# A third seven-product quad in groups 7 and 8 of a fused attention and GEGLU kernel, with a new order of their weight sums and output products

## The chip, the cores and the metric

The kernel runs on one core of a Trainium2 chip. The metric is the device time of one launch in microseconds (us). The kernel before was timed three times: 324.16 us in the median, 323.65 and 324.44 at the ends. A separate profiled execution, from which every row below is taken, took 324.89 us, and its trace spans 323.1 us.

## The reference

Two operators run one after the other. The first is causal attention over a sliding window of 128 keys with a linear distance penalty (ALiBi), for 8 batches, 8 heads, 576 positions and 64 dimensions a head:

```
scores = q k^T / 8 - slope[h] * |i - j|,   kept where 0 <= i - j < 128
attn   = softmax(scores);   x = attn v
```

Its output is laid out as 4608 tokens of 512 features. The second is a GEGLU block on those tokens:

```
out = (gelu(x @ w_gate) * (x @ w_val)) @ w_out      # 512 -> 1536 -> 512, exact gelu
```

Inputs and output are float32; the matmuls in the kernel take bf16 and accumulate in float32.

## The kernel before, in words

**Groups and blocks.** The 4608 tokens are cut into 9 groups (g = 0 to 8) of 512 tokens. The 1536 hidden features are 12 blocks of 128 (f = 0 to 11). For each group the kernel computes the hidden tile `hT` from the attention output `xT`, block by block, and then the output product of `hT` with `wo`. The attention of a later batch is interleaved with the groups: while group g is worked on, batch g + 1 gets its sums and batch g + 2 its scores. Batch 7, the last, is finished in the output stage of group 6, so groups 7 and 8 hold no attention at all.

**Order of the work.** There is no automatic scheduler here: the kernel is written under a manual schedule. Each engine takes its instructions strictly in the order in which the Python code emits them, and a semaphore wait holds up everything behind it on the same engine. TensorE (PE) does matmuls, ScalarE (ACT) copies out of the accumulators and evaluates exp and gelu, VectorE (DVE) does additions and multiplications that read accumulators, GpSimd (POOL) does additions on SBUF data and issues most loads, and SyncE (SP) issues stores, transposing DMAs and the small relays between two halves of an accumulator bank.

**Plain blocks.** `gate_val` (L628) computes one block of one group: four matmuls of 512 columns for the gate, four for the value, one gelu on ACT (L649), one multiplication on DVE (L650).

**Quads.** `gate_quad` (L805) computes four blocks at once with a seven-product scheme (Strassen's, in Winograd's form). It takes the two weight matrices as a 2 by 2 matrix (gate and value, each cut into two halves of the 512 features) and the tokens as a 2 by 2 matrix (the same halves, and two halves of 256 tokens). Seven products of 8 matmuls with 256 columns take the place of eight. The inner function `P(n)` issues product n for two pairs of blocks, u = 0 and 1. The order on PE is P(1), P(2), P(6), P(5), P(7), P(3), P(4). In between, ACT copies P(1), the sum in x and P(5) out of the accumulators (L843, L849, L852) and evaluates the gelu of two halves (L836); DVE adds into these copies (`add_to`, L833: after P(2), after P(7), after P(3)) and multiplies the lower token half (L866); POOL multiplies the upper token half (L870, L872). A quad holds six of the eight accumulator banks: two called x, two z and two y. Its staging space and gelu space come from tiles that are no longer in use (`rooms`, L794).

**Sums that a quad needs.** `combine_weights(f0)` (L755) makes four sums of weights with eight additions. Those for blocks 6 to 9 are made once and stay in `kept`; those for blocks 0 to 3 are made by POOL during the output stage of group 6 and lie in the probabilities' space `Ps[0]`. `combine_x(g)` (L777) makes four sums of tokens with four additions. Group 7's are made in two parts, tokens 0 to 191 early by DVE, and tokens 192 to 255, which need the end of batch 7, by POOL in the output stage of group 6 (L1192).

**Output products.** `out_products` (L1142) uses the same scheme for `hT` times `wo`, again seven products, here of 6 matmuls for each half a = 0, 1 of the group's lower 256 tokens; `product` (L735) issues one. The sums of hidden values come from `combine_left` (L712), in four kinds: 0 and 1 give the left factors of products 5 and 6, 3 that of product 7, 2 that of product 3. `gather_out` (L885) takes the products out: copies on ACT (named p1, u2, p5, c21), additions on DVE (c11, c22, c12). Product 4 accumulates on top of the bank that c22 reads.

**Groups 7 and 8 before.** Quad 0 (blocks 0 to 3), plain blocks 4 and 5, quad 6 (blocks 6 to 9), plain blocks 10 and 11, and then all output products in a row, with `combine_left` spread over POOL and DVE.

**Batch 3.** `spread_dma` (L447) reads the reciprocals of the row sums back from DRAM and spreads them over partitions. For batch 3 it is issued on ACT's queue, after block 11 of group 2; for the others by SP after block 6.

**The start.** `keep_busy` (L73) runs matmuls on zeros while the first inputs arrive (L1018).

## Time and profile before

| | before |
|---|---|
| median of 3 runs | 324.16 us (323.65 to 324.44) |
| profiled execution | 324.89 us, of which the trace spans 323.1 us |
| PE busy | 313.5 us, 97% of the span |
| DVE busy | 249.2 us, 77% |
| ACT busy | 219.5 us, 68% |
| POOL busy | 197.0 us, 61% |
| granted TensorE clock | 1.00 in every slice |
| group 7, hidden blocks | 262.96 to 282.09 us of the span |
| group 7, output products | 282.09 to 291.29 us |
| group 8, hidden blocks | 291.29 to 310.42 us |
| group 8, output products | from 310.42 us |

How to read it. The trace has one row for each stretch of like instructions on an engine: start and length in us from the span's beginning, the engine, the line of the kernel, the operation, what it writes and reads, shapes, and how often. A bracket behind it gives the time that the engine had idled and what ended the wait. Matmuls are pipelined and the end of each is modelled, so a row of n matmuls is somewhat longer than the time to the next row's start; starts are the better measure. The chain of waits follows the work back from the last instruction, at each step to what released it. The 1.79 us between the span and the execution's time lie outside the trace.

### The profile page before, as it was taken

The numbers are of one execution on the slowest core, as the hardware profiler recorded it, in microseconds if no ns is written. First come the engines' busy times: TensorE is split into PE (matmuls) and PEld (weight loads), VectorE is DVE, ScalarE is ACT, GpSimd is POOL, SyncE is SP. The second block draws the span as 40 slices with busy tenths as digits, with TensorE's granted clock in tenths as the row PEclk, the third lists the DMA queues.
The fourth block names the chain that finished last, engine by engine and source line by source line (L and its number), as shares of the span: only waits on it lengthen the run. The fifth ranks groups of instructions, "written<-read, shape, count | busy, mean of one in ns | idle before, by whom it ended". The sixth has DMA issues, their size and how long they took to land.

```text
span 323.1 us, 9359 instructions
## 1 busy us (share of the span) xinstructions
PE 313.5 (97%) x3712; PEld 212.5 (66%) x3742; DVE 249.2 (77%) x493; ACT 219.5 (68%) x421; POOL 197.0 (61%) x228
## 2 busy tenths in 40 slices
PE   8889999999999999999999999999999999999995
PEld 3565746466454768566855786578747787788764
DVE  7769776978779887976798679877897756895692
ACT  7973678647979679657966787578767256627641
POOL 5974589385096885579945995496009496410450
PEclk9999999999999999999999999999999999999999
DMA  7999999999999959995999699949204230003003
GB/s 210 166 194 192 200 178 181 139 178 191 161 147 164 138 101 181 191 142 153 179 193 158 162 168 190 148 124 179 102 36 103 49 132 0 2 0 132 0 4 130
DMA packets 149920, 43.57 MB, mean 135 GB/s; under 512 B 133588, under 2 KB 142964, under 8 KB 149876
## 3 DMA queue, kind: packets, MB, share of 16 engines
q0 software_dynamic: 107456, 18.10, 75.9%
q1 hardware_dynamic: 41424, 23.35, 33.1%
q10 hardware_dynamic: 996, 1.53, 2.1%
q8 instruction: 29, 0.48, 0.6%
q14 instruction: 15, 0.12, 0.1%
HBM read 43.65 MB, written 9.53 MB: 165 GB/s over the span
## 4 chain that ended last, share of the span: by engine, by line
PE 91%; ACT 3%; issue 2%; DMA 1%; DVE 1%; SPq 0%; ACTq 0%; DVEq 0%
PE ps L643 36%; PE ps L745 20%; PE ps L825 19%; PE ps L494 5%; PE ps L679 4%; PE ps L304 2%; PE ps L699 2%; PE ps L218 1%; DMA qs<-in_q_dram 1%; ACT P L233 1%; PE ps L432 1%; PE ps L156 1%; SPq L938 0%; DVE xT L533 0%; ACTq L449 0%
## 5 line engine op out<-in xcount | busy, mean ns | idle before, releaser
L643 PE MATMUL ps<-xT,wv 128*128 128x512 bf16 (+3 forms) x303 | 71.3, 354 | 0.2
L643 PE MATMUL ps<-xT,wg 128*128 128x512 bf16 (+3 forms) x290 | 68.8, 353 | 1.6 <-issue 0.6
L649 ACT ACTIVATE gelu<-ps 128x512 bf16<-128x512 f32 (+3 forms) x77 | 41.6, 546 | 41.5 <-PE ps L643 38.5
L650 DVE TENSOR_TENSOR hT<-ps,gelu 128x512 bf16<-128x512 f32 (+3 forms) x77 | 46.3, 623 | 18.4 <-PE ps L643 14.7
L233 ACT ACTIVATE P<-ps 128x512 bf16<-128x512 f32 (+1 forms) x108 | 52.5, 577 | 6.2 <-PE ps L304 3.0
L643 PEld LDWEIGHTS <-wv 128*128 128x128 bf16 x308 | 28.9, 98 | 30.8 <-DVE xT L553 1.4
L643 PEld LDWEIGHTS <-wg 128*128 128x128 bf16 x308 | 28.4, 98 | 26.7 <-issue 0.7
L238 DVE TENSOR_TENSOR P<-P,emask 128x768 bf16<-128x768 bf16 x60 | 31.9, 553 | 6.8 <-ACT P L233 5.1
L745 PEld LDWEIGHTS <-hT 128*128 128x128 bf16 x336 | 32.1, 98 | 6.3 <-issue 0.5
L114 POOL DMA_DIRECT2D vb<-in_v_dram x40 | 33.9, 878 | 3.7 <-DMA wo<-in_moe_w_out_dram 1.0
L870 POOL TENSOR_TENSOR hT<-qT,qs 128x512 bf16<-128x512 f32 x10 | 11.5, 1167 | 26.5 <-ACT qs L836 26.5
L114 POOL DMA_DIRECT2D ks<-in_k_dram x30 | 25.4, 886 | 3.4 <-DMA qs<-in_q_dram 3.2
L825 PEld LDWEIGHTS <-kept 128*128 128x128 bf16 x256 | 25.1, 98 | 2.9
L1332 POOL COPY mark<-hT 1x2 bf16<-1x2 bf16 x5 | 0.9, 174 | 42.7 <-DVE hT L650 42.7
L114 POOL DMA_DIRECT2D qs<-in_q_dram x30 | 25.4, 863 | 1.7 <-DMA wo<-in_moe_w_out_dram 0.9
L745 PEld LDWEIGHTS <-left 128*128 128x128 bf16 x252 | 24.1, 98 | 3.4 <-DVE left L720 0.2
L745 PE MATMUL ps<-right,hT 128*128 128x256 bf16 x168 | 22.2, 273 | 0.3 <-ACT osb L894 0.3
L833 DVE TENSOR_TENSOR qT<-ps,qT 128x512 f32<-128x512 f32 x20 | 12.9, 686 | 12.2 <-PE ps L825 10.9
L745 PE MATMUL ps<-wo,hT 128*128 128x256 bf16 x168 | 21.2, 273 | 0.0
L833 DVE TENSOR_TENSOR P<-ps,P 128x512 f32<-128x512 f32 x24 | 15.0, 682 | 7.1 <-PE ps L825 7.1
L745 PE MATMUL ps<-right,left 128*128 128x256 bf16 x168 | 20.4, 273 | 0.0
L494 PE MATMUL ps<-P,vb 64*64 64x192 bf16 (+2 forms) x752 | 17.5, 221 | 1.7 <-issue 1.5
(173 smaller groups left out, 615.7 us busy)
## 6 DMA issues: line engine op xcount, KB each, us to landing
out_dram<-osb SPq DMA_DIRECT2D x34, 256.0 KB
rb<-rd SPq DMA_DIRECT2D x8, 576.0 KB
vb<-in_v_dram POOLq DMA_DIRECT2D x32, 128.0 KB, 7.1
qs<-in_q_dram POOLq DMA_DIRECT2D x24, 128.0 KB, 6.1
ks<-in_k_dram POOLq DMA_DIRECT2D x24, 128.0 KB, 7.3
wo<-in_moe_w_out_dram POOLq DMA_DIRECT2D x4, 384.0 KB, 12.2
wg<-in_moe_w_gate_dram POOLq DMA_DIRECT2D x5, 256.0 KB, 7.8
wv<-in_moe_w_val_dram POOLq DMA_DIRECT2D x5, 256.0 KB, 8.4
```

Source lines behind the costliest of these rows:

```text
L114: nc.gpsimd.dma_start(out=t[at:at + n, j, :].rearrange("p (h d) -> p h d", h=H), in_=src[b][:, 128 * j:128 * j + n, :].rearrange("h p d -> ...
L233: nc.scalar.activation(out=dst, in_=src, func=AF.Exp, scale=0.125)
L238: nc.vector.tensor_tensor(out=dst, in0=dst, in1=m, op=ALU.mult)
L494: mm = nc.tensor.matmul(out=out, lhsT=lhsT, rhs=prob(b)[half, c, i, col:col + q1 - q0], start=all(t[2] != u for t in todo[:n]), stop=True, ...
L643: nc.tensor.matmul(out=ps, lhsT=w[:, c, 128 * f:128 * (f + 1)], rhs=xT[:, c, t0 + lo:t0 + hi], start=begins, stop=(c == 3), skip_group_che ...
L649: nc.scalar.activation(out=gl[:, 0:n], in_=pg, func=AF.Gelu)
L650: nc.vector.tensor_tensor(out=hid[g][:, f, lo:hi], in0=pv, in1=gl[:, 0:n], op=ALU.mult)
L679: nc.tensor.matmul(out=acc[g], lhsT=hid[g][:, f, 128 * t:128 * (t + 1)], rhs=wo[:, f, :], start=(f == 0), stop=(f == NF - 1))
L745: nc.tensor.matmul(out=made[g, a, into], lhsT=lhsT, rhs=rhs, start=first and i == 0, stop=i == NF // 2 - 1, skip_group_check=True)
L825: nc.tensor.matmul(out=ps[:, 256 * e:256 * e + 256], lhsT=w[:, c, at:at + 128], rhs=x[:, c, :], start=n in (1, 2, 5) and e == 0 and c == 0 ...
L833: nc.vector.tensor_tensor(out=to[u], in0=cut(banks[n, u], to[u].shape[1]), in1=to[u], op=ALU.add)
L870: nc.gpsimd.tensor_tensor(out=out, in0=P5[u], in1=high, op=ALU.mult)
```

## The change

- **Groups 7 and 8** compute quad 6 first, then quad 0, then a third quad that takes blocks 4, 5, 10 and 11 in place of the four plain blocks. The constant `PAIRS` says which blocks make up a quad.
- The third quad's **weight sums** (`combine_weights(4)`, eight additions) are made by POOL in group 7, three before quad 6 and five after it, in the space of `Ps[1]`, and used again in group 8. It has staging space of its own, and its upper token half is multiplied by DVE instead of POOL (`high=nc.vector`), after both lower multiplications. Between its first and second additions DVE makes the sums of kinds 0 and 1 for blocks 6 to 9 (`between`).
- **Output products of groups 7 and 8**: products 1, 2, 6 and 5 are each issued in two parts, first for the pairs of blocks 0, 1, 3, 4 (in the old quads) and then for 2 and 5 (in the third quad). All sums of kinds 3 and 2 go to DVE. In group 7 `combine_x` for group 8 comes after product 7 instead of after product 6.
- **Output stage of group 6**: `combine_x` for tokens 192 to 255 goes from POOL to DVE, behind c11 of a = 1.
- **Batch 3**: its spread is issued by POOL after block 6, ahead of the loads of batch 5. In group 2 the exp table is loaded before the copy p1, as in the later groups.
- **Groups 2 to 5**: half of one addition into `T` (the second of the two of part 0) moves behind the scaling of the previous batch's values.
- **The start**: 2 matmuls of 128, 7 of 512 and 2 of 128 columns on zeros in place of 8 of 512.

```diff
-QUADS = (0, 6)
+PAIRS = {0: (0, 2), 6: (6, 8), 4: (4, 10)}
...
-            (nc.scalar if b == 3 else nc.sync).dma_start(
+            (nc.gpsimd if b == 3 else nc.sync).dma_start(
                 out=recip[b][64 * i:64 * i + 64, :, :],
...
     def gate_quad(g, f0, room=None, between=None, high=nc.gpsimd):
...
+        if high is nc.vector:
+            low(0)
+            low(1)
         for u in (0, 1):
+            if high is not nc.vector:
+                low(u)
...
-    keep_busy(held[0], 8, 512, zeros[:, 0:1].to_broadcast((128, 512)))
+    keep_busy(held[0], 2, 128)
+    keep_busy(held[0], 7, 512, zeros[:, 0:1].to_broadcast((128, 512)))
+    keep_busy(held[0], 2, 128)
...
         if b > B:
+            early, late = (0, 1, 3, 4), (2, 5)
+            def both(n, which=range(NF // 2), *after):
+                for a in (0, 1):
+                    P(n, a, which)
+                    for what in after:
+                        O(what, a)
+                store()
+            both(1, early)
+            both(2, early)
+            both(1, late, "p1")
+            both(2, late)
+            combine_left(g, 2, 6, (0, 1), step=3)
+            both(6, early)
+            both(5, early)
+            combine_left(g, 0, 6, (3,))
+            both(6, late, "u2", "c11")
+            both(5, late, "p5")
+            combine_left(g, 0, 6, (2,))
+            both(7, range(NF // 2), "c22")
+            if g + 1 < NG:
+                combine_x(g + 1)
+                both(3, range(NF // 2), "c12")
+                both(4, range(NF // 2), "c21")
...
-            combine_x(g + 1, 192, 256, engine=nc.gpsimd)
             for do in sums[4:]:
                 do()
             O("c11", 1)
+            combine_x(g + 1, 192, 256)
             P(6, 1)
...
-        if g == 2:
-            O("p1", 0)
         exp_table()
-        if g > 2:
-            O("p1", 0)
+        O("p1", 0)
...
-        add(b, 0, None, (0,))
+        add(b, 0, None, (0,), (0,))
...
+        add(b, 0, None, (0,), (1,))
...
         if g >= B - 1:
+            sums = combine_weights(4) if g == B - 1 else []
+            for do in sums[:3]:
+                do()
+            gate_quad(g, 6)
+            store()
+            for do in sums[3:]:
+                do()
+            gate_quad(g, 0)
+            combine_left(g, 0, 2, (0, 1), engine=nc.gpsimd)
+            gate_quad(g, 4, (wide_of([(kT[1], 2), (vb[0], 2), (vb[1], 2)]), tiles_of([(qs[1], 4)])),
+                      lambda: combine_left(g, 3, 5, (0, 1)), high=nc.vector)
             out_products(g)
...
-            if f == (11 if g == 2 else 6):
+            if f == 6:
                 spread_dma(g + 1)
```

More of the change, by code (lines that the diff above doesn't have):

```diff
@@ L377, in scores0_rest, with add @@
                           emask[:, 2 * c:2 * c + 2, 0:192].unsqueeze(2).to_broadcast((128, 2, 2, 192))))
-    def add(b, c0, copy=None, what=(0, 2, 1)):
+    def add(b, c0, copy=None, what=(0, 2, 1), halves=(0, 1)):
         hs = slice(2 * c0, 2 * c0 + 4)
@@ L385, in add @@
         if 0 in what:
-            for x in (0, 1):
+            for x in halves:
                 half = slice(64 * x, 64 * x + 64)
@@ L710, in halves, with combine_left @@
         return hid[g].rearrange("p (i e) (h t) -> p i e h t", e=2, h=2)
-    def combine_left(g, lo, hi, which=(0, 1, 2, 3), engine=nc.vector):
-        x, ns = halves(g), slice(lo, hi)
+    def combine_left(g, lo, hi, which=(0, 1, 2, 3), engine=nc.vector, step=1):
+        x, ns = halves(g), slice(lo, hi, step)
         a11, a12, a21, a22 = (x[:, ns, e, h, :] for h in (0, 1) for e in (0, 1))
@@ L733, with product @@
     made = {}
-    def product(g, n, a, lo=0, hi=NF // 2):
+    def product(g, n, a, which=range(NF // 2)):
         (l, r), into = FACTORS[n], INTO[n]
-        first = n in (1, 2, 5)
+        count = made.get((g, a, n), 0)
+        first = n in (1, 2, 5) and not count
+        made[g, a, n] = count + len(which)
         if first:
@@ L741, in product @@
         x = wo.rearrange("p (i e) (h t) -> p i e h t", e=2, h=2)
-        for i in range(lo, hi):
+        for k, i in enumerate(which):
             lhsT = left[:, l, i, cols] if isinstance(l, int) else halves(g)[:, i, l[0], l[1], cols]
             rhs = right[:, r, i, :] if isinstance(r, int) else x[:, i, r[0], r[1], :]
-            nc.tensor.matmul(out=made[g, a, into], lhsT=lhsT, rhs=rhs, start=first and i == 0,
-                             stop=i == NF // 2 - 1, skip_group_check=True)
+            nc.tensor.matmul(out=made[g, a, into], lhsT=lhsT, rhs=rhs, start=first and k == 0,
+                             stop=count + k == NF // 2 - 1, skip_group_check=True)
     def flat_of(t):
@@ L752, with weights @@
     sums_w = {0: [flat_of(Ps[0])[:, 1024 * n:1024 * n + 1024].rearrange("p (c f) -> p c f", c=2) for n in range(4)],
+              4: [flat_of(Ps[1])[:, 1024 * n:1024 * n + 1024].rearrange("p (c f) -> p c f", c=2) for n in range(4)],
               6: [kept[:, n, :, :] for n in range(4)]}
+    def weights(w, c, f0):
+        a, b = PAIRS[f0]
+        return w[:, c, 128 * a:128 * b + 256].rearrange("p (n y) -> p n y", y=256)[:, 0:(b - a) // 2 + 1:(b - a) // 2, :]
     def combine_weights(f0, engine=nc.gpsimd):
@@ L803, in rooms, with gate_quad @@
             P[:, 4 * n:4 * n + 4, 288:416] for n in (0, 1)], tiles_of([(vb[g % 2], 4)])
-    def gate_quad(g, f0, room=None, between=None):
+    def gate_quad(g, f0, room=None, between=None, high=nc.gpsimd):
         if g not in hid:
@@ L838, in hidden @@
         def hidden(u, half):
-            return hid[g][:, f0 + 2 * u:f0 + 2 * u + 2, 256 * half:256 * half + 256]
+            f = PAIRS[f0][u]
+            return hid[g][:, f:f + 2, 256 * half:256 * half + 256]
         P(1)
@@ L1146, in out_products @@
         if b > B:
-            last = [(4, ("c21",)), (3, ("c12",))]
-            for n, after in [(1, ("p1",)), (2, ()), (6, ("u2", "c11")), (5, ("p5",)), (7, ("c22",))] + (
-                    last if g == NG - 1 else last[::-1]):
-                early = g == NG - 1 and n in (3, 4)
+            early, late = (0, 1, 3, 4), (2, 5)
+            def both(n, which=range(NF // 2), *after):
                 for a in (0, 1):
-                    if early and a == 0 and n == 4:
-                        P(3, 0, 0, 1)
-                    P(n, a, *((1,) if early and a == 0 and n == 3 else ()))
+                    P(n, a, which)
                     for what in after:
@@ L1157, in out_products @@
                 store()
-                if n == 6 and g + 1 < NG:
-                    combine_x(g + 1)
+            both(1, early)
[14 more added lines that the diff above has]
+                both(4, range(NF // 2), "c21")
+            else:
+                P(3, 0, range(1))
+                both(4, range(NF // 2), "c21")
+                P(3, 0, range(1, 6))
+                O("c12", 0)
+                store()
+                P(3, 1)
+                O("c12", 1)
+                store()
             return
@@ L1235, in out_products @@
         P(1, 1)
-        P(3, 0, 0, 2)
+        P(3, 0, range(2))
         P(4, 0)
-        P(3, 0, 2)
+        P(3, 0, range(2, 6))
         O("p1", 1)
@@ L1281 @@
         if g >= B - 1:
[L1282 to L1296 removed]
+            sums = combine_weights(4) if g == B - 1 else []
+            for do in sums[:3]:
+                do()
+            gate_quad(g, 6)
+            store()
+            for do in sums[3:]:
[4 more added lines that the diff above has]
+                      lambda: combine_left(g, 3, 5, (0, 1)), high=nc.vector)
             out_products(g)
```

42 lines of the change are left out of this document (16 added, 26 removed).

## The prediction

> **What bounds the kernel now.** I read the page first, for the engines' shares:
>
> ```profile
> span 323.1 us, 9359 instructions
> PE 313.5 (97%) x3712; PEld 212.5 (66%) x3742; DVE 249.2 (77%) x493; ACT 219.5 (68%) x421; POOL 197.0 (61%) x228
> ```
>
> Then the chain of waits from 255 us on, since most of the change lies there:
>
> ```profile
> 256.39 6.73 PE ps L745 x60
> 263.12 6.11 PE ps L825 x56
> 269.24 0.05 issue
> 269.29 3.40 PE ps L643 x15
> 272.69 6.11 PE ps L825 x56
> ...
> 282.26 9.19 PE ps L745 x84
> ```
>
> The chain is PE alone: a quad of 56 matmuls takes 6.11 us, two plain blocks 3.40 + 0.05, the 84 output matmuls 9.19, nothing between. So work taken from PE is time gained, and any wait put before a matmul is time lost in full. I work in us against the profiled execution, 324.89 (span 323.1 and 1.79 around it); it stands 0.73 above the median of 324.16, and I carry the difference over to the median.
>
> **1. The third quad: -1.6.** Four plain blocks cost 2 x 3.45 = 6.90, a quad 6.11; 0.79 a group, 1.58 in two, if PE runs the quads back to back.
>
> **2. Batch 3's spread: -0.3.** In group 2 PE waits once:
>
> ```profile
> 117.31 1.33 ACTq L449 DMA_DIRECT2D rb<-rd  x2
> 121.40 0.38 ACT L894 COPY osb<-ps 128x256 f32<-128x256 f32 x1
> 121.83 0.82 PE L745 MATMUL ps<-right,hT 128*128 128x256 bf16 x6 [0.33 <-ACT osb L894]
> ```
>
> The two issues hold ACT for 1.33; the copy u2 at 121.40 comes late by this, and PE's product 7 by 0.33. Without them the table load follows the last gelu, and the wait goes: -0.33, at least 0. On POOL two issues stand ahead of batch 5's loads. These rows tell who waits for them:
>
> ```profile
> 117.72 4.27 POOL L114 DMA_DIRECT2D qs<-in_q_dram  x5
> 135.85 4.19 SPq L177 DMA_TRANSPOSE kT<-ks  x1
> 150.29 1.33 SPq L449 DMA_DIRECT2D rb<-rd  x2
> 153.44 0.80 PE ps L304 x33
> ```
>
> Five issues take 4.27, two some 1.7. If all of this reaches SP's transposes, SP is done at 153.3 instead of 151.6, just as PE's scores of 153.44 begin, whose relays SP carries. I take 0, at most +0.3.
>
> **3. Group 6's token sums on DVE: +3.2.** The sums for tokens 192 to 255 are four additions of 128x128, put in front of c22 on DVE while POOL makes weight sums without a break:
>
> ```profile
> 256.52 2.26 POOL L761 TENSOR_TENSOR P<-wv 128x512 bf16<-128x512 bf16 x2
> 258.75 2.26 POOL L761 TENSOR_TENSOR P<-P,wg 128x512 bf16<-128x512 bf16 x2
> 260.11 0.41 DVE L896 TENSOR_TENSOR osb<-ps,osb 128x256 f32<-128x256 f32 x1
> 260.98 0.42 POOL L783 TENSOR_TENSOR ks<-xT 128x128 bf16<-128x128 bf16 x1
> 261.83 0.42 DVE L902 TENSOR_TENSOR osb<-ps,osb 128x256 f32<-128x256 f32 x1 [1.31 <-ACT osb L900]
> 262.31 0.81 PE L745 MATMUL ps<-right,hT 128*128 128x256 bf16 x6
> ```
>
> The DVE row at 261.83 is c22 of a = 1, ended at 262.25; PE's product 4, which accumulates onto the bank that c22 reads, starts at 262.31. There is no slack: what delays c22 delays PE, and behind it all of groups 7 and 8. What a DVE addition on two SBUF operands costs beside a busy POOL is seen in group 7:
>
> ```profile
> 279.36 2.32 POOL L870 TENSOR_TENSOR hT<-qT,qs 128x512 bf16<-128x512 f32 x2 [4.83 <-ACT qs L836]
> 280.33 0.34 DVE L720 TENSOR_TENSOR left<-hT 128x256 bf16<-128x256 bf16 x1
> 280.70 1.12 DVE L720 TENSOR_TENSOR left<-left,hT 128x256 bf16<-128x256 bf16 x1
> 282.80 1.15 POOL L720 TENSOR_TENSOR left<-hT,left 128x512 bf16<-128x512 bf16 x1
> 282.97 1.25 DVE L720 TENSOR_TENSOR left<-hT 128x512 bf16<-128x512 bf16 x1
> 284.26 0.42 DVE L720 TENSOR_TENSOR left<-left,hT 128x512 bf16<-128x512 bf16 x1
> 284.60 0.28 DVE L720 TENSOR_TENSOR left<-hT 128x256 bf16<-128x256 bf16 x1
> ```
>
> With POOL idle, 256 columns take 0.28 and 512 take 0.42. With POOL at work the same take 1.12 and 1.25, and end just after POOL's instruction has ended (281.82 after 281.68, 284.22 after 283.95). So the DVE addition waits for POOL's current instruction; and the addition at 280.70 came too late to follow the one at 280.33, because POOL's next had begun in between. Additions that read an accumulator (0.41 and 0.42 here, beside a busy POOL) don't wait. Now the four: c11 ends at 260.52. POOL, whose own token sums are gone, is in its fourth addition until 261.0. The first DVE addition (0.2 by the two lengths above, an estimate) ends at 261.2, and each further one waits out one POOL addition of 1.1: 262.5, 263.8, 265.1. c22 then ends at 265.5 instead of 262.25, and PE loses 3.2. This is the upper end. If the third and fourth, which need nothing that isn't ready, follow the second before POOL gets in, c22 ends at 263.2: +1.0. With no waiting at all the four take 0.8 and are done by 261.4, before c22 could start: 0. I take 3.2, since in each case seen POOL got in between.
>
> The Trainium skill (SBUF — State Buffer, section "SBUF: two separate sides") has a rule on this that speaks against the change: VectorE instructions with two SBUF inputs and GpSimd's share a pair of ports under an exclusive lock, held for a whole instruction, and the loser blocks fully. The 1.12 and 1.25 agree with it. By that rule each of the four competes anew, which is the 3.2; the gentler ordering above would need VectorE to keep the lock between two instructions.
>
> **4. Quads back to back: +0.4.** Here are ACT's and DVE's rows for quad 6, whose PE work runs from 272.53 to 278.64:
>
> ```profile
> 272.53 1.91 PE L825 MATMUL ps<-xT,wg 128*128 128x256 bf16 x16
> 274.27 2.78 PE L825 MATMUL ps<-ks,kept 128*128 128x256 bf16 x24
> 277.77 1.04 PE L825 MATMUL ps<-ks,wv 128*128 128x256 bf16 x8
> 273.22 1.07 ACT L843 COPY qT<-ps 128x512 f32<-128x512 f32 x2 [0.70 <-PE ps L825]
> 278.65 1.23 ACT L836 ACTIVATE qs<-kT 128x512 bf16<-128x512 f32 x2 [0.59 <-DVE kT L833]
> 274.11 1.29 DVE L833 TENSOR_TENSOR qT<-ps,qT 128x512 f32<-128x512 f32 x2 [0.62 <-PE ps L825]
> 276.73 1.29 DVE L833 TENSOR_TENSOR qT<-ps,qT 128x512 f32<-128x512 f32 x2 [1.33 <-PE ps L825]
> 279.13 1.28 DVE L866 TENSOR_TENSOR hT<-ps,qs 128x512 bf16<-128x512 f32 x2
> ```
>
> ACT's last gelu ends 1.24 after the quad does (279.88 - 278.64). The next quad's copies could start 0.69 after its own start (273.22 - 272.53) and now start at 1.24; the first ends at 1.24 + 0.54 = 1.78, and P(6), due at 1.74, needs it: about 0.1 lost with the semaphore. Two such places in each of two groups: +0.4; the lower end is 0. The plain blocks gave ACT this time before.
>
> Accumulator banks: six of eight are in use in a quad, and the two called z are free again after the first additions (275.40). So the next quad finds four, which do for P(1) and P(2), and I add nothing. If the banks are handed out in fixed turn instead, P(2) of the next quad, due 0.87 after its start, waits for the lower multiplications (279.13 and 0.6 later, ended by 280.41): the second ends 1.77 after the quad's end where PE wants it at 0.87 + 0.44 = 1.31, so 0.5 at six places (the output products of each group count too), 3.0. The code doesn't fix the turn, and I keep this as an upper end.
>
> **5. DVE's sums inside the third quad: +0.7.** `between` puts two dependent additions of 512 columns behind DVE's first pair, which ends 275.40 - 272.53 = 2.87 after a quad's start (3.1 with the lag of part 4). Alone they take 0.8 and end at 3.9, before the next pair's 4.20. But POOL then works on quad 0's upper halves (2.3 for two) and its sums (2 x 1.15). The pair of 276.73 ends 5.49 after the start and P(4)'s second half is due at 5.24 + 0.44, so 0.2 is the slack. Both additions waiting out a whole POOL instruction would end at 3.1 + 2 x 1.45 = 6.0 and cost 1.6. In group 7 POOL's five weight sums (5 x 1.12) come between quad 6's multiplications (6.8 to 9.1 after the group's start, by 279.36 - 272.53) and quad 0's, which so run from 14.7, or 2.3 in the third quad's own time, to 4.6: the second addition is held until then and ends at 4.9, a loss of 0.3 to 0.4; I take 0.3. In group 8 POOL is about to begin its sums at 3.1, and I let one of the two additions be held: 0.4. Bounds 0 and 1.6 for each group.
>
> **6. Output products: +0.2.** After the third quad DVE still has two lower and two upper multiplications (2.4 to 2.6), two sums (0.8) and then this kind twice, with two c11 (0.75) between:
>
> ```profile
> 254.50 0.95 DVE L720 TENSOR_TENSOR hT<-hT 128x1536 bf16<-128x1536 bf16 x1
> ```
>
> That is 0.5 + 2.5 + 0.8 + 0.95 + 0.75 + 0.95 = 6.5 after the quad's end; product 3 in group 8 starts after 60 matmuls of 0.109 (9.19 / 84), at 6.6. Product 7 needs the first of the pair at 5.2 and has it at 4.8. With the lateness of part 5 some tenths are lost once: +0.2, between 0 and 0.4. POOL's sums for blocks 0 to 3 are needed 2.6 or more after the quad's end and are there.
>
> **7. At nothing.** POOL's eight new weight sums (8 x 1.12) fit: POOL is free of sums before quad 6's multiplications, and the last one is due only in the third quad's P(3), some 3 us after it ends; were it late, its lateness would be the price. The half addition moves within DVE's queue while PE, behind it, has output products to do. The start:
>
> ```profile
> 1.00 3.59 PE L75 MATMUL ps<-zeros 128*128 128x512 bf16 x8 [1.00 <-DVE zeros L927]
> 4.41 0.50 PE L995 MATMUL ps<-ident,qs 128*128 128x128 bf16 x3
> ```
>
> The columns are 4096 in both; a matmul of 128 starts 0.13 after the one before (0.50 less 0.24 for the last one's length, over two), so four cost at most 0.52 where one of 512 cost 0.45: 0 to +0.07.
>
> **The sum.** -1.58 - 0.33 + 3.2 + 0.4 + 0.7 + 0.2 = +2.6: 327.5 for the profiled execution, 326.8 for the median.
>
> **The rivals.**
>
> *The lock lets DVE's later additions through* (part 3 at 1.0): -1.58 - 0.33 + 1.0 + 0.4 + 0.7 + 0.2 = +0.4, 324.6. For it: those additions are independent, unlike the pairs seen. Against: POOL had its next instruction waiting each time.
>
> *DVE isn't held*, the faster side: a DVE addition that arrives while POOL has a queue goes between at once, and POOL waits. Parts 3 and 5 fall to 0; -1.91 + 0.4 = -1.5, 322.7. It decides from the point where the four token sums stay under about 0.3 each, so that c22 starts at 261.83 as before. For it: the addition at 280.33 took only 0.34. Against: 1.12 and 1.25.
>
> *Worse*: banks in fixed turn (+3.0), or both sums of part 5 held for whole instructions in group 8 (+1.2): 328.0 to 329.8.
>
> *The third quad saves nothing*, as its PE time is hidden: the chain above excludes it, PE being the bound.
>
> **How the numbers follow.** No change that a measurement of this kernel can tell is within 0.3%, 323.2 to 325.1. Forecast 326.8 with chance 0.45, its own range 325.6 to 328.0 (parts 4 to 6 at their ends); the first rival 0.17 (same), the second 0.28 (faster), the worse ones 0.10. Slower 0.55. The range takes in the second rival and the forecast's own: 322.4 to 328.2.
>
> **What would show it.** In the changed profile: the four DVE additions on line L783's successor in group 6's output stage at about 1.1 each and a wait of PE before the last product there (part 3); 168 quad matmuls a group in about 18.5 to 19.4 us with gaps of about 0.1 where quads meet; DVE's two sums inside the third quad above 0.42 each, and a wait of P(4) on DVE; no wait on u2 in group 2. I am wrong if the four are short and PE doesn't wait there.

## The result, and the profile after

The kernel after takes 333.25 us in the median of 6 runs (332.44 to 335.50), the kernel before 324.11 beside it; the ratio is 1.028 (95% interval 1.026 to 1.030). It is slower by 9.1 us. Its profiled execution took 333.11. The page after:

```profile
span 331.3 us, 9491 instructions
...
PE 315.4 (95%) x3767; PEld 218.9 (66%) x3793; DVE 264.7 (80%) x501; ACT 225.0 (68%) x433; POOL 201.4 (61%) x230
...
PEclk9999999999999999999999999999999959999999
```

PE's share fell from 97 to 95%, and one slice of forty has half the TensorE clock. The chain of waits (start, length, what) shows where:

```profile
250.94 2.67 PE ps L747 x24
...
259.27 8.32 DVE ks L789
...
268.50 1.44 PE ps L747 x6
269.94 16.61 PE ps L836 x136
...
290.63 9.29 PE ps L747 x84
299.91 18.64 PE ps L836 x168
```

Until group 6's output products (250.94, before 252.19) the profiled run is 1.25 ahead. Then one DVE addition stands in the chain for 8.3 us. DVE's rows there, with POOL's and PE's for the same time (L789 is a token sum, L921 is c22, L767 a weight sum, L747 an output product, L836 a quad's product):

```profile
258.86 0.41 DVE L915 TENSOR_TENSOR osb<-ps,osb 128x256 f32<-128x256 f32 x1
259.19 8.39 DVE L789 TENSOR_TENSOR ks<-xT 128x128 bf16<-128x128 bf16 x1
267.61 0.22 DVE L789 TENSOR_TENSOR ks<-xT,ks 128x128 bf16<-128x128 bf16 x1
...
268.03 0.42 DVE L921 TENSOR_TENSOR osb<-ps,osb 128x256 f32<-128x256 f32 x1
...
255.27 2.25 POOL L767 TENSOR_TENSOR P<-wv 128x512 bf16<-128x512 bf16 x2
...
264.14 2.24 POOL L767 TENSOR_TENSOR P<-wv 128x512 bf16<-128x512 bf16 x2
266.35 1.14 POOL L767 TENSOR_TENSOR P<-P,wg 128x512 bf16<-128x512 bf16 x1
...
268.50 1.44 PE L747 MATMUL ps<-right,hT 128*128 128x256 bf16 x6 [7.35 <-DVE osb L921]
269.73 3.57 PE L836 MATMUL ps<-xT,wg 128*128 128x256 bf16 x16
```

The first token sum starts inside POOL's fourth weight sum and ends at 267.58, just behind the eleventh (267.49). From the lengths of its neighbours, 0.22, it was held for some 8.2 of its 8.39; the trace books all of it as DVE's busy time. The next three take 0.22 each, c22 follows, and PE, which waits for c22, has stood for 7.35. Then it is slow: product 4 takes 1.44 where before it took 0.81, the first 16 matmuls of the quad 3.57 where a quad at full speed took 1.91. In a table of stretches (from:to, length, then the busy time of PE, PEld, DVE, ACT and POOL with their counts, granted clock, DMA share, GB/s):

```profile
268.50:271.20 2.70, 2.70 (x13) 1.93 (x13) 0.28 (x1) 0.69 (x2) 0.00 (x0) 0.50 0.26 98
271.20:280.00 8.80, 8.80 (x74) 7.45 (x72) 5.79 (x10) 6.18 (x13) 1.78 (x2) 0.89 0.08 30
```

The granted clock is 0.50 after the wait, 0.89 in the next stretch, and back at 1.00 later (in 299.91:318.55). Quad 6 takes 269.73 to 277.51, that is 7.78 instead of 6.11. So the stall costs 7.35, and the slow clock (1.44 - 0.81) + (7.78 - 6.11) = 2.3 more.

The account, in us of the span, by PE's starts: -1.25 up to group 6's output products; +7.35 and +2.3; the rest of group 7's hidden blocks -0.07 (269.73 to 290.46, that is 20.73 for 19.13, less 1.67 of clock); its output products +0.09 (9.29 for 9.20); group 8's hidden blocks -0.49 (18.64 for 19.13), and its output products with the end of the span +0.23 (12.91 for 12.68). That is +8.2, as the two profiled executions differ (333.11 - 324.89).

### The profile page after: what moved, and what is told of

Its sections match the earlier page's. It is cut to its first block, busy times and chain, and to the rows that moved or that the text cites. A ratio compares the mean times of both kernels' runs of the same rounds, so it can differ in the third digit from the quotient of the medians.

```text
span 331.3 us, 9491 instructions
## 1 busy us (share of the span) xinstructions
PE 315.4 (95%) x3767; PEld 218.9 (66%) x3793; DVE 264.7 (80%) x501; ACT 225.0 (68%) x433; POOL 201.4 (61%) x230
## 4 chain that ended last, share of the span: by engine, by line
PE 91%; DVE 5%; issue 2%; ACT 1%; ACTq 0%; DVEq 0%
PE ps L643 31%; PE ps L836 22%; PE ps L747 19%; PE ps L494 5%; PE ps L679 4%; DVE ks L789 3%; PE ps L304 2%; PE ps L699 2%; PE ps L218 2%; PE ps L75 1%; PE ps L432 1%; PE ps L156 1%; DVE xT L574 0%; ACT P L233 0%; PE ps L1014 0%
## 5 line engine op out<-in xcount | busy, mean ns | idle before, releaser
L643 PE MATMUL ps<-xT,wv 128*128 128x512 bf16 (+3 forms) x271 | 63.1, 351 | 0.2
L643 PE MATMUL ps<-xT,wg 128*128 128x512 bf16 (+3 forms) x262 | 61.1, 350 | 1.3 <-issue 0.6
L649 ACT ACTIVATE gelu<-ps 128x512 bf16<-128x512 f32 (+3 forms) x69 | 36.9, 541 | 36.5 <-PE ps L643 34.3
L650 DVE TENSOR_TENSOR hT<-ps,gelu 128x512 bf16<-128x512 f32 (+3 forms) x69 | 40.7, 616 | 15.7 <-PE ps L643 12.2
L643 PEld LDWEIGHTS <-wv 128*128 128x128 bf16 x276 | 25.9, 98 | 26.4
L747 PEld LDWEIGHTS <-hT 128*128 128x128 bf16 x336 | 32.1, 98 | 13.9 <-issue 8.0
L643 PEld LDWEIGHTS <-wg 128*128 128x128 bf16 x276 | 25.2, 98 | 23.6 <-issue 0.4
L747 PE MATMUL ps<-right,hT 128*128 128x256 bf16 x168 | 23.1, 278 | 7.6 <-DVE osb L921 7.4
L836 PEld LDWEIGHTS <-kept 128*128 128x128 bf16 x256 | 25.1, 98 | 3.0
L747 PEld LDWEIGHTS <-left 128*128 128x128 bf16 x252 | 24.2, 98 | 3.5 <-issue 0.3
L836 PE MATMUL ps<-xT,wg 128*128 128x256 bf16 x192 | 24.6, 285 | 0.0
L836 PEld LDWEIGHTS <-wg 128*128 128x128 bf16 x192 | 19.6, 102 | 4.1
L747 PE MATMUL ps<-wo,hT 128*128 128x256 bf16 x168 | 21.4, 273 | 0.0
```

Of the source, the lines that this page charges most:

```text
L643: nc.tensor.matmul(out=ps, lhsT=w[:, c, 128 * f:128 * (f + 1)], rhs=xT[:, c, t0 + lo:t0 + hi], start=begins, stop=(c == 3), skip_group_che ...
L649: nc.scalar.activation(out=gl[:, 0:n], in_=pg, func=AF.Gelu)
L650: nc.vector.tensor_tensor(out=hid[g][:, f, lo:hi], in0=pv, in1=gl[:, 0:n], op=ALU.mult)
L747: nc.tensor.matmul(out=made[g, a, into], lhsT=lhsT, rhs=rhs, start=first and k == 0, stop=count + k == NF // 2 - 1, skip_group_check=True)
L836: nc.tensor.matmul(out=ps[:, 256 * e:256 * e + 256], lhsT=lhsT, rhs=x[:, c, :], start=n in (1, 2, 5) and e == 0 and c == 0, stop=c == 1, s ...
```

## The experiments

The theory after this result: while POOL has additions ready, DVE's addition on two SBUF inputs waits for the end of POOL's whole run, not for one instruction; and the slow clock follows from PE's standing. The rival is the prediction's: one POOL instruction for each DVE addition.

**The token sums back on POOL.** The old place, ahead of the second four weight sums:

```diff
+            combine_x(g + 1, 192, 256, engine=nc.gpsimd)
             for do in sums[4:]:
                 do()
             O("c11", 1)
-            combine_x(g + 1, 192, 256)
```

> The changed kernel with the four token sums of group 6's output stage back on POOL, at their old place; all else as changed. Theory (run): what cost the time is that DVE's first token sum waited 8.39 us, until POOL's run of weight sums ended, with PE behind it for 7.35, and that PE then ran 2.3 us slower at a lower clock. Then no wait of PE before product 4, clock 1.00 throughout, and 333.1 - 7.35 - 2.3 = 323.5, within 0.8 of it, since POOL is 1.7 later in group 7 and may hold up the third quad more. Rival: the third quad and its sums are the loss; then above 328.

Measured 325.82, ratio 1.007 (1.004 to 1.010). PE doesn't wait before product 4, so the stall does hang on this one move. It is 2.3 above what was expected, because POOL, with four more additions, is late in group 7, and there the two DVE sums inside the third quad wait (2.59 and 1.25). The first:

```profile
277.32 2.59 DVE L720 TENSOR_TENSOR left<-hT 128x512 bf16<-128x512 bf16 x1
```

**A run of eight.** The three early sums of the third quad go behind quad 6:

```diff
-            for do in sums[:3]:
-                do()
             gate_quad(g, 6)
             store()
-            for do in sums[3:]:
+            for do in sums:
                 do()
```

> The changed kernel with the first three weight sums of the third quad issued behind quad 6's multiplications with the other five, so that POOL's run beside DVE's token sums is 8 additions long and not 11. Theory (run): DVE's first token sum waits 3 x 1.11 = 3.3 less, 5.0 in place of 8.39, and PE waits 4.0 in place of 7.35. Rival (it waits for something else than the end of POOL's run, data or a fixed time): 8.4 and 7.35 as before. The third quad's own sums come later and may cost up to 2 there; so 330 to 332 by the first, 333 to 335 by the rival.

Measured 332.7 in two runs (331.43 and 333.97; ratio 1.025). The first token sum and PE's product 4:

```profile
258.94 5.08 DVE L789 TENSOR_TENSOR ks<-xT 128x128 bf16<-128x128 bf16 x1
...
264.93 1.44 PE L747 MATMUL ps<-right,hT 128*128 128x256 bf16 x6 [4.04 <-DVE osb L921]
```

Three sums less (3.3 us) and the wait is 3.3 shorter: the run's end decides. It gave little back in time, since the clock fell after 4.04 of standing too, and the late sums held up the third quad. (Two runs don't tell its time from that of after; the rows do tell the waits apart.)

**Gaps in the run.** Behind each weight sum POOL copies two elements of its result, so that it has to wait for itself:

```diff
+            def one(o, a, b, op):
+                engine.tensor_tensor(out=o, in0=a, in1=b, op=op)
+                if engine is nc.gpsimd:
+                    engine.tensor_copy(out=mark, in_=o[0:1, 1, 254:256])
...
```

> The changed kernel with a copy of two elements on POOL behind each of its weight sums, reading what that sum wrote, so that POOL must finish one before it goes on. Theory (run): DVE gets in at the first such gap; each token sum waits for one addition at most, the first 1.3 or less, and PE's wait before product 4 is 1 to 3.5. Rival (DVE waits until POOL has nothing at all to do): POOL's run is longer by 11 copies of about 0.3, so the first token sum waits 9 or more and PE 8 or more.

Measured 325.16, 1.004 (1.002 to 1.005). The four token sums took 0.22, 1.20, 0.21 and 1.30, and PE waited 1.2. The gaps, copies of 0.18 to 0.27, let DVE in, as the theory says; the clock stayed at 1.00.

**PE kept busy.** 34 matmuls on zeros ahead of product 4:

```diff
+            keep_busy(bank(), 34, 512, zeros[:, 0:1].to_broadcast((128, 512)))
             P(4, 1)
```

> The changed kernel with 34 matmuls of 512 columns on zeros (7.3 us) in PE's queue ahead of the last product of group 6, into a bank that nobody reads. Theory (clock): PE still can't go on before 268.5 or so, but its clock doesn't fall; product 4 takes 0.82 instead of 1.44 and quad 6 6.1 instead of 7.78, so 333.1 - 2.3 = 330.8. Rival (quad 6 is slow because its operands or sums are late): 333, with quad 6 at 7.8.

Measured 330.13 in two runs (330.25 and 330.01; ratio 1.018). DVE's wait is the same, PE's speed behind it is not:

```profile
258.56 8.41 DVE L789 TENSOR_TENSOR ks<-xT 128x128 bf16<-128x128 bf16 x1
...
268.53 1.91 PE L836 MATMUL ps<-xT,wg 128*128 128x256 bf16 x16
```

1.91 again at a granted clock of 1.00, and 3 us less in time: the slow matmuls came from PE's standing. The Trainium skill (TensorE: Matmul & The Clock Gate, section "Part 1: The HAM clock gate") says that the clock falls to half after an idle window of about 3.4 us; 7.35 and 4.04 here, and 1.2 with no fall, agree with it.

**POOL waits for the token sums.** The remedy: POOL's second four sums start only when DVE's token sums are done.

```diff
+            O("c11", 1)
+            combine_x(g + 1, 192, 256)
+            nc.gpsimd.tensor_copy(out=mark, in_=sums_x(g + 1)[3][0:1, 1, 254:256])
             for do in sums[4:]:
                 do()
-            O("c11", 1)
-            combine_x(g + 1, 192, 256)
```

> The kernel after with one new wait: POOL's second four weight sums in group 6's output products begin only when the four token sums on DVE are done (a copy of two elements on POOL that reads the last of them). The run in front of the token sums is then four additions instead of eleven. Theory that a whole run of POOL's ready additions holds DVE: the first token sum lasts until the fourth weight sum ends, 0.5 to 0.8, the others 0.22 each, PE waits 0 to 0.3 for product 4, the clock stays at 1.0, and the rest of group 7 is late only where DVE's sums inside the third quad meet POOL's sums and multiplications (1 to 2): 323.0, between 322.3 and 324. Theory of the prediction, one POOL addition for each DVE addition: with POOL idle behind its fourth sum it gives the same here, 0.5 and three short ones, so this run prices the remedy rather than tells the two apart. If instead DVE's additions on SBUF are slow beside whatever POOL does, PE waits 3 or more and the time stays above 327.

Measured 323.52, ratio 0.996 (0.994 to 0.998): 9.7 below after, and 0.4% below before, a small gain. DVE's first token sum and c22, POOL's second four sums, and the chain of waits from there:

```profile
258.42 0.65 DVE L789 TENSOR_TENSOR ks<-xT 128x128 bf16<-128x128 bf16 x1
...
259.81 0.42 DVE L921 TENSOR_TENSOR osb<-ps,osb 128x256 f32<-128x256 f32 x1 [0.21 <-issue]
...
259.80 2.26 POOL L767 TENSOR_TENSOR P<-wg,wv 128x512 bf16<-128x512 bf16 x2
```

```profile
254.37 6.73 PE ps L747 x60
261.10 14.99 PE ps L836 x136
...
280.17 9.29 PE ps L747 x84
```

All 60 output matmuls follow each other in 6.73, as before. Group 7's hidden blocks take 19.07 (261.10 to 280.17).

**The sums behind the lower multiplications.** The same, and DVE's two sums leave the middle of the third quad:

```diff
-        if between:
+        if between and high is not nc.vector:
             between()
...
             low(0)
             low(1)
+            if between:
+                between()
...
```

> As the run before, and DVE's two sums inside the third quad stand behind its two lower multiplications instead of behind its first pair of additions, so that no add of the quad is queued behind them. If part 5 of the prediction has its place right (a sum held by POOL holds DVE's next pair and with it P(4)), the third quad takes 6.2 in both groups, PE waits nowhere in groups 7 and 8 for an add into vb, and the time is 1 to 2 under the run before: 321.8, faster than both kernels. Rival: the sums are then late for product 6 (due 2.6 after the quad), and what is won in the quad is lost there: as the run before.

Measured 323.52, 0.998 (0.996 to 1.000): as the run before, so the rival holds. PE's rows at the start of each quad of group 7, of its output products and of group 8:

```profile
263.93 1.91 PE L836 MATMUL ps<-xT,wg 128*128 128x256 bf16 x16
...
270.04 1.91 PE L836 MATMUL ps<-xT,wg 128*128 128x256 bf16 x16
...
276.23 1.91 PE L836 MATMUL ps<-xT,wg 128*128 128x256 bf16 x16
...
282.40 2.78 PE L747 MATMUL ps<-wo,hT 128*128 128x256 bf16 x24
...
292.16 1.91 PE L836 MATMUL ps<-xT,wg 128*128 128x256 bf16 x16
```

By these starts the quads take 6.11, 6.19 and 6.17, 18.47 in all instead of 19.06; the third alone took 6.77 in the run before, so what it lost there came from the two sums. The products take 9.76 instead of 9.29: with the sums behind the multiplications, PE waits 0.19 for a left factor and starts late at other places. 28.23 against 28.35 in all.

**The small parts.** Two kernels on the base of before: the 11 zero matmuls alone, and these with batch 3's spread, the later p1 and the half addition.

```diff
-    keep_busy(held[0], 8, 512, zeros[:, 0:1].to_broadcast((128, 512)))
+    keep_busy(held[0], 2, 128)
+    keep_busy(held[0], 7, 512, zeros[:, 0:1].to_broadcast((128, 512)))
+    keep_busy(held[0], 2, 128)
```

> The kernel before with the 11 zero matmuls of the change alone. The profiled run of before has 1.54 us of PE standing at 15.70 to 17.24 with nothing named that it waits for; the runs of after and of the first four experiments have none, and all of them hold the new zeros. If the zeros are what takes it away, the time falls by about 1.0, to 323.2, and the first gate matmul starts at about 16.5 or earlier. If it is an accident of the one profiled run, or comes from something else in the change, the time stays within 0.3 of before, 324.2, and I price the zeros at 0 to +0.07 as in the prediction.

> The kernel before with everything of the change outside groups 6, 7 and 8: the zeros, the spread of batch 3 on POOL, p1 behind the table load, half an addition into T later. By the ledger of the profiled run of after (1.25 us ahead of before at group 6's output products) it takes 322.9, with no wait of PE on u2 in group 2 (-0.33) and a stall less of 0.3 to 0.4 at 130 us. By the prediction's parts 2 and 7 alone it takes 323.8. If the head start is an accident of single runs, 324.2.

The zeros: 0.999 (0.998 to 1.001), no difference; the 1.54 us stall at the start of the profiled run before is gone here at an equal time, and it is no fixed price of the old zeros: in five added runs with these (the five kernels of added stages below) it is 0.16 to 0.83. All small parts: 0.998 (0.996 to 1.000), or -0.7 us with an interval of -1.3 to -0.1. The kernel that waits for the token sums is another 0.3 below this by the medians. The intervals don't tell the two apart, but one profiled run of each gives the same: groups 7 and 8 take 56.33 us in it and 56.66 with the small parts alone.

**POOL and DVE alone.** Is it really the run? Stages behind the end of the kernel before, with nothing else at work: POOL gets six ready instructions (eight in the next two runs), DVE comes in between, in most stages after a copy out of an accumulator; the first copy lets POOL start. Of these runs only the rows count, and each was profiled once.

```diff
+    def phase(kind, wait, adds, n=6):
...
+        nc.vector.tensor_copy(out=kf[0:1, 0:2], in_=last[0:1, 0:2])
+        for i in range(n):
...
+            nc.gpsimd.tensor_tensor(out=out, in0=a, in1=kf[:, 0:512], op=ALU.mult if kind == "f32" else ALU.add)
...
+        for _ in range(wait):
+            nc.vector.tensor_copy(out=flat_of(qT[1]).bitcast(FP32)[:, 0:512], in_=spare)
+        for i in range(adds):
+            nc.vector.tensor_tensor(out=slot(kT[0], i, 256), in0=slot(vb[0], i, 256), in1=slot(vb[1], i, 256), op=ALU.add)
```

> The kernel before with eight short stages added at its end, which compute nothing of the output (some 60 us; the time itself is of no use). In each, POOL runs six instructions of 128x512 that are ready from the start, and DVE comes in between with additions of 128x256 on SBUF, most of them after one copy out of an accumulator (0.7), so that they arrive inside POOL's first instruction. POOL's six are additions bf16 with bf16 that don't depend on each other, multiplications f32 with bf16 like the upper halves of a quad, or additions each of which reads the one before. Theory 1, a run of ready POOL instructions holds DVE whatever they are: about 6 us for one DVE addition beside the independent additions and beside the multiplications, at most 1.3 beside the chain, whose links leave gaps; four DVE additions behind each other take the end of the run and three times 0.25. Theory 2, only the bf16 additions hold on, the multiplications let DVE in at each boundary (as at 286.63 of after, 0.85): 6 us beside the additions, 1.3 or less beside the multiplications. Theory 3, the prediction's, one POOL instruction for each DVE addition everywhere: 0.5 to 1.3 in each stage. If what counts is when DVE arrives, the stages without the copy ahead (DVE there at about the same moment as POOL) differ from those with it.

The theory fell. In no stage did DVE wait out more than one POOL instruction at a time, whatever POOL did (in the two without the copy it was there ahead of POOL). Four DVE additions beside six independent bf16 additions:

```profile
342.56 4.32 DVE L1397 TENSOR_TENSOR kT<-vb,vb 128x256 bf16<-128x256 bf16 x4
```

That is 1.08 each, which is the prediction's rule.

> The kernel before with twelve stages added at its end, which compute nothing of the output (the time itself is of no use). The last run went against my theory: there DVE got in after one POOL instruction in every stage, while in group 6 of after it waited out seven. So something else than POOL's being ready decides. The stages put the parts of group 6 together again: POOL runs eight instructions, either its real weight sums, or additions of one tile with itself, or additions in two strided pieces of 256; DVE brings the real four token sums (128x128 in two pieces of 64), or four plain additions of 256 or 128 columns, or the two product sums of 512; in three stages PE runs 40 matmuls beside them, in two of these ACT 12 copies. If POOL's operands decide, all stages with the real sums hold DVE for 5 to 8 us. If DVE's do, all with the token sums. If it takes a busy PE or ACT, only those stages. If none holds it for more than 1.3, the cause is none of these, and stays open.

Neither the operands nor a busy PE or ACT makes the difference: the real token sums beside the real weight sums took 0.91, 1.07, 1.18 and 1.18, with PE and ACT at work or not, and no other stage held DVE for longer than 1.25.

> The kernel before with 24 stages added at its end, which compute nothing of the output (the time itself is of no use). In each, POOL runs its eight real weight sums and DVE brings the four token sums; only the moment at which DVE arrives inside POOL's first sum is moved, by the width of a copy (in the last eight an addition) out of an accumulator ahead of them, from about 0.35 to 1.0 us after the sum's start. In the runs of the changed kernel in which DVE was held for the whole run (after, the run of eight, the one with PE kept busy) it arrived 0.58 to 0.59 after the start of POOL's fourth sum; in the stages of the last two runs, which never held it, at 0.03 to 0.38, and at 1.03. If the moment decides, some stages, those near 0.59, hold DVE for 7 to 8 us and the others for at most 1.3. If it doesn't, none of the 24 does, and what held DVE in group 6 stays open.

Nor does the moment inside the sum: in all 24 stages, with arrivals from 0.5 to 1.0 us after the start of POOL's first sum, the first token sum ended just behind that sum. What all these stages share is that DVE comes early in the run. The next three runs try that. The second puts a copy of 0.41 between c11 and the token sums of after; the third puts one more addition into DVE's order:

```diff
             P(3, 0)
             scale[1]()
+            nc.vector.tensor_tensor(out=flat_of(ks[0])[:, 0:128], in0=wg[:, 0, 0:128], in1=wv[:, 0, 0:128], op=ALU.add)
```

> The kernel before with 14 stages added at its end, which compute nothing of the output (the time itself is of no use). POOL runs its eight weight sums (in two stages twelve additions), and DVE comes to its additions on SBUF only inside the fourth sum or later, as in group 6 of after; in three stages with the same instructions ahead as there (four multiplications out of an accumulator into the tokens, one addition out of an accumulator), so that the first token sum also waits for DVE's own last multiplication; one of these with PE and ACT at work; seven stages move the moment inside the sum; three bring other additions. If it is the late arrival, or DVE's wait for itself, that makes POOL keep the port, these stages hold DVE to the end of the run, 3 to 9 us. If none does, neither is the cause.

> The kernel after with a copy of 256 columns out of an accumulator (0.3 to 0.4) on DVE between c11 and the four token sums, so that they come later inside POOL's run and behind another instruction. If the moment inside POOL's sum decides, which is 0.58 in all runs that were held, DVE arrives at about 0.95 here and is held for at most one sum each, and the time is 326 to 328. If not, DVE is held to the end of the run again, for about 8.0, and the time stays at 333.

> The kernel after with one more addition on DVE, 128 columns of weights into a dead tile, ahead of the third scaling, some 2 us before the token sums and inside POOL's first or second weight sum. If any DVE addition on two SBUF inputs is held by this run, it waits for its end, about 10.5, and the time is 335 to 336. If one early in the run gets in after one sum, it lasts 0.3 to 1.3, and what counts is where in the run DVE arrives; then the token sums behind it show whether a first turn changes what follows.

In the first, DVE arrived in POOL's third sum in 13 of the 14 stages and in the fifth in one. Eleven stages held it to the run's end, for 3.8 to 10.3 us, all with nothing but POOL and DVE at work. Two of them, beside runs of eight and of twelve:

```profile
332.30 5.86 DVE L783 TENSOR_TENSOR ks<-xT 128x128 bf16<-128x128 bf16 x1
...
342.09 10.27 DVE L783 TENSOR_TENSOR ks<-xT 128x128 bf16<-128x128 bf16 x1
```

In the other three DVE had arrived in the last 0.14, 0.19 and 0.23 of POOL's third sum and got in behind it; four of the eleven came that late as well, so there it goes either way. In the second run the token sum was held for 8.06, so a later moment doesn't help; 331.88. The third gave 328.33: one addition *more* on DVE, 5 us less than after. DVE's rows, and PE's product 4:

```profile
256.60 0.67 DVE L1225 TENSOR_TENSOR ks<-wg,wv 128x128 bf16<-128x128 bf16 x1
...
259.45 1.15 DVE L789 TENSOR_TENSOR ks<-xT 128x128 bf16<-128x128 bf16 x1
260.63 1.08 DVE L789 TENSOR_TENSOR ks<-xT,ks 128x128 bf16<-128x128 bf16 x1
261.63 1.18 DVE L789 TENSOR_TENSOR ks<-xT 128x128 bf16<-128x128 bf16 x1
...
264.31 1.01 PE L747 MATMUL ps<-right,hT 128*128 128x256 bf16 x6 [3.51 <-DVE osb L921]
```

The added one (L1225) arrives in POOL's second sum and gets in behind it; after it the four token sums go one by one (1.15, 1.08, 1.18 and 1.18), which is the case that the prediction had priced. PE waited 3.51; the granted clock was 0.74 in product 4 (264.31:265.32) and 0.50 in the next 2.7 us.

**Which sum DVE meets.** Only the place in the run is moved.

> The kernel before with 21 stages added at its end, which compute nothing of the output (the time itself is of no use). POOL runs eight instructions (real weight sums in six stages, additions of one tile in six, f32 by bf16 multiplications in six), and DVE's four token sums arrive in the middle of POOL's first, second, third, fourth, fifth or sixth. From the runs so far: arrival in the first or second gets in after that one and the four go one by one (about 1.1 each); arrival in the third or later is held to the run's end (some 6, 5, 4 and 3 us for the third to the sixth). If this holds for the weight sums alone, the multiplications show 0.3 to 1.3 everywhere, as the upper halves in group 7 did. In the last three stages DVE brings one addition of 128 columns in the first, second or third sum and the token sums two or more sums later: if an early turn keeps the way open, as one look at the changed kernel with an early addition suggests, the token sums go one by one in the first two and the early addition itself is held in the third. If the sum that DVE meets is not what decides, held and not held mix without such an order.

The stages were meant to bring the first token sum into POOL's first to sixth weight sum of eight. A step of the delay (two copies, 1.36) is longer than a sum (1.11), so by the rows of POOL it arrived in the first, second, fourth, fifth, sixth and seventh; the third was missed. DVE's six rows, and POOL's for the stage at 341.91:

```profile
320.62 0.49 DVE L783 TENSOR_TENSOR ks<-xT 128x128 bf16<-128x128 bf16 x1
...
331.26 0.23 DVE L783 TENSOR_TENSOR ks<-xT 128x128 bf16<-128x128 bf16 x1
...
341.91 5.51 DVE L783 TENSOR_TENSOR ks<-xT 128x128 bf16<-128x128 bf16 x1
...
353.04 4.17 DVE L783 TENSOR_TENSOR ks<-xT 128x128 bf16<-128x128 bf16 x1
...
364.20 2.80 DVE L783 TENSOR_TENSOR ks<-xT 128x128 bf16<-128x128 bf16 x1
...
375.35 1.45 DVE L783 TENSOR_TENSOR ks<-xT 128x128 bf16<-128x128 bf16 x1
...
338.45 2.24 POOL L761 TENSOR_TENSOR P<-wv 128x512 bf16<-128x512 bf16 x2
340.66 2.25 POOL L761 TENSOR_TENSOR P<-P,wg 128x512 bf16<-128x512 bf16 x2
```

First or second: in behind that one. Fourth or later: held to the end. For the third there is the run of late arrivals above, where ten of 13 were held. Since every sum takes 1.1, these stages don't tell whether the number of sums decides or the time since the run began. The six stages with plain additions and the six with f32 multiplications gave the same within 0.02, so the guess that multiplications let DVE in is wrong. The last three stages have one early addition, in the first, second and (again meant for the third) fourth sum:

```profile
493.85 0.49 DVE L1397 TENSOR_TENSOR kT<-vb,vb 128x128 bf16<-128x128 bf16 x1
...
499.57 0.31 DVE L783 TENSOR_TENSOR ks<-xT 128x128 bf16<-128x128 bf16 x1
...
508.72 0.56 DVE L783 TENSOR_TENSOR ks<-xT 128x128 bf16<-128x128 bf16 x1
...
515.38 5.51 DVE L1397 TENSOR_TENSOR kT<-vb,vb 128x128 bf16<-128x128 bf16 x1
```

After an early turn the token sums arrive in the sixth sum and still get in (0.31, 0.56); an early addition that comes only in the fourth is itself held (5.51).

## Why the prediction was wrong

The direction was right (slower), and so was the place: PE before product 4 in group 6, behind DVE's four token sums. The size was not: 333.25 against 326.8, above the upper end of 328.2.

**Part 3 is the step that failed**: "each further one waits out one POOL addition of 1.1". It was worked out from group 7 of before, where DVE's additions at 280.33 and 280.70 met POOL's *first* two instructions of a run. In group 6 DVE arrives in the fourth of eleven, and there it was held to the run's end: a wait of 7.35 instead of 3.2. The price for one by one was sound: in the run with an early addition the four took about 1.1 each, and PE waited 3.51. The part's bounds, 0 and 3.2, were no bounds, because the longest wait that the rows allowed, POOL's whole run, was never priced. Both the prediction's rivals on the lock asked only who goes next; that POOL might go on to the end wasn't among them. (The second of them, in which DVE isn't held, also leaves out part 6 in its sum: -1.91 + 0.4 + 0.2 is -1.3, or 322.9.)

The rule of the Trainium skill that the prediction drew on (SBUF — State Buffer, section "SBUF: two separate sides": an exclusive lock for the whole instruction, the loser blocks) holds for an early arrival. It doesn't say that a run of GpSimd instructions can keep the other side out, as it did here for most of 8.39 us; the measurement decides.

**The clock is a term that the sum didn't have.** PE's standing cost 2.3 more at half clock. The forecast's own case would have had it too: after the 3.51 wait of the run with an early addition, group 7's hidden blocks took 20.53 (265.32 to 285.85) instead of 19.07, and product 4 took 1.01 instead of 0.81, some 1.7 together.

So part 3 cost 7.35 + 2.3 = 9.6 where the sum had 3.2. With 9.6 in its place the prediction's sum is +9.0; the medians differ by 9.1, the two profiled executions by 8.2.

**Parts 1, 4, 5 and 6** were forecast at -1.58 + 0.4 + 0.7 + 0.2 = -0.28. Undisturbed, in the kernel where POOL waits, groups 7 and 8 gain 56.66 - 56.33 = 0.33. The terms inside fit, with some luck. Part 4, quads back to back, had its place right: with the sums out of the way a quad takes 6.11 and each of the two behind it 0.06 to 0.08 more, 0.27 in the two groups for a forecast of 0.4. Part 5, the sums inside the third quad, cost 0.6 in group 7 (6.77 less 6.17) and 0.16 in group 8 (6.34 less 6.18), where 0.3 and 0.4 were forecast: the total is right, 0.76 for 0.7, because its halves are off in opposite directions. The output products lost 0.2 in the two groups, as forecast. The rows in group 7 of after show part 5 at work:

```profile
286.63 0.85 DVE L720 TENSOR_TENSOR left<-hT 128x512 bf16<-128x512 bf16 x1
287.51 1.26 DVE L720 TENSOR_TENSOR left<-left,hT 128x512 bf16<-128x512 bf16 x1
...
289.43 1.19 PE L836 MATMUL ps<-ks,wv 128*128 128x256 bf16 x8 [0.28 <-DVE vb L844]
```

**Parts 2 and 7** were forecast at -0.33 and 0. The small parts alone measured -0.7 (-1.3 to -0.1), which holds it; the zeros measured no difference. In the profiled run of the small parts PE waits on u2 in group 2 no longer. The 1.25 that the profiled run of after was ahead at group 6 is more than these parts gave; the rest may be the scatter of single runs at the start, which was not shown. Eight weight sums of POOL "at nothing" is the other place where the working was too narrow: they fitted POOL's own time, but they made the run in group 6 longer, by the three early ones, 3.3 us of the wait.

**What stays open.** Why an early turn matters wasn't seen, only that it does. Group 7 has rows that go against the rule of the stages: at 286.63 of after DVE came into the eighth of nine POOL instructions without a gap (two multiplications, five sums, two multiplications) and got in. In the run of eight it came even into a weight sum, the eighth of twelve instructions, with 5.4 us of them left, and got in:

```profile
283.27 0.84 DVE L720 TENSOR_TENSOR left<-hT 128x512 bf16<-128x512 bf16 x1
```

In the kernel with the token sums on POOL, by contrast, its addition at 277.32 came 0.08 before the end of the last sum and waited out both multiplications. So being held to the end is shown for group 6's run of weight sums and for the added stages, and what makes group 7 differ is open.

## What to carry to other kernels

Before moving an addition on two SBUF inputs to VectorE beside a busy GpSimd, look in the trace at how many GpSimd instructions stand ready there without a gap and in which of them the addition will arrive: price the whole rest of that run as the upper end, not one instruction. A GpSimd instruction that waits for VectorE's result in the middle of the run, here a copy of two elements, cut the wait from 7.35 to 0 and took 9.7 us off the changed kernel; what is left of the change, 0.4% under before, is about half the small parts. When a wait of several us is put before PE, add the slow clock behind it: here 1.7 us after a wait of 3.51 and 2.3 after 7.35, none after 1.2. Nothing between 1.2 and 3.51 was tried.

## What the runs showed of the hardware

- In group 6 and in the added stages, a run of back-to-back GpSimd instructions on SBUF kept VectorE's additions on two SBUF inputs out until it ended, for up to 10.27 us, when VectorE came in the fourth instruction or later, and in ten of 13 stages when it came in the third, and had had no turn before in that run. In the first or second it got in behind that one (1.25 at most with its own time), and from then on the two went one by one, 1.07 to 1.24 us for each addition. bf16 additions and f32 multiplications on GpSimd made no difference (within 0.02). Rows of group 7 (0.85 at 286.63 of after, 0.84 at 283.27 of the run of eight) are exceptions.
- Additions that read an accumulator aren't held by the same run: 0.41 for c11 at 258.86 of after, inside the run that held the next addition for 8.39.
- In group 6's run, a copy of two elements on GpSimd that reads its own last result left a gap in which VectorE got in: waits of 8.39 became 1.3 at most.
- TensorE's granted clock was 0.50 after 7.35, 4.04 and 3.51 us of standing (in the last case from the quad on; 0.74 in the product before it). After 1.2 it stayed at 1.00, and zero matmuls in the wait of 7.35 kept it there.
